# Eight tiles in place of five with a seven-product second matmul, and the scores before them moved up

## The chip, the cores and the metric

The kernel runs on one core of a Trainium2 chip. The metric is the device time of one execution in microseconds (us). Before the change three runs gave 2065.69, 2065.81 and 2067.15 us, with a median of 2065.81.

## What is computed

Four batches of channel attention feed a two-layer network. With `B, N, C = 4, 6080, 256` and `DFF = 2048`, the reference is, cut to what matters:

```python
qn = q / (norm(q, axis=1) + 1e-6)           # per batch and channel
kn = k / (norm(k, axis=1) + 1e-6)
s = kn.transpose(0, 2, 1) @ qn / tau        # C x C scores, a sum over all N rows
a = softmax(s)
x = v @ a                                   # N x C per batch
h = x @ w_in
out = maximum(0.01 * h, h) @ w_out
```

## The kernel before

**Tiles.** The rows of a batch are cut into six tiles of two halves, 512 columns a half in the first four and 496 in the last two. Tiles are numbered 0 to 23 over the batches, so batch 3 is tiles 18 to 23. Each tile runs over eight pairs of 128-wide blocks of `DFF` (`NPAIR`), numbered 0 to 7.

**First product.** `v @ (a @ w_in)` is taken in one: the 256x256 softmax is first multiplied into `w_in` (`w_pair`, then `w_parts`), and the result, split in a high and a low half, goes to DRAM (`w_dram`) and comes back pair by pair (`w_load`). Products with it are made in seven block products in place of eight (`block_product`, L1069), each in three passes of halves: 21 matmuls a pair. From tile 6 on all halves are 2-byte floats. On the way ScalarE copies a block from PSUM (`taken`, L1112) and VectorE adds a second one to it (`add`, L1106); that sum must be read out of bank `ps_z` before the next product adds to `ps_z`.

**Second product.** In plain tiles `ffn_out` (L1386) multiplies the four activated blocks of a pair by `w_out` in eight block products, 24 matmuls a pair. In the tiles of `FAST`, 18 to 22, `fast_slot` writes out a pair by hand: there the second product too is made in seven block products (`fast_out`, L1206), 21 matmuls a pair. Its operands are sums of activated blocks, which GpSimd's accumulating DMAs make (`sums_start`), and sums of blocks of `w_out`, made once into the tile `spare` (`wo_sums`). VectorE makes the low halves (`low`, L1167; in plain tiles `leaky`, L1099). A step that belongs to the next tile lies in pair 1 of such a tile: `v_scale` gathers the largest value of the next `v` (L163 to L177) and turns it into scales (`find` and `v_found`, L191 to L973).

**Scores.** Each batch's scores are summed over 48 chunks of rows while earlier tiles run. Batch 3's chunks are already scaled by the norms: `unit` on VectorE (L297), a cast to the high half on ScalarE (L302), the low half on VectorE (L306), then four matmuls (`product`, L336), two of 512 columns and two of 256, into the banks `ps_s` and `ps_y`. The norms themselves come from squares summed ahead, which fill `spare` until then. Batch 2's norms need a reciprocal of 258 columns (`wide_inverse`, L444).

**Order.** The program is one stream; each engine's own order is as recorded. Work that isn't a tile's own stands in lists per engine (`put`), and `slot(queue, room)` at fixed places of a pair records from a list what fits into `room`, an assumed length in us. Chunks, norms and sums enter the lists at pairs numbered from the start (`at`). Batch 2's scores begin at pair 48 over 28 pairs, batch 3's at pair 100 over 25 pairs; each batch's products with `w_in` follow them.

## Time and profile before

| | us |
|---|---|
| median of three runs | 2065.81 |
| profiled execution | 2066.83 |
| span of its trace | 2064.86 |
| TensorE busy | 2048.8 (99%) |
| VectorE busy | 1691.7 (82%) |
| ScalarE busy | 1496.6 (72%) |
| GpSimd busy | 256.2 (12%) |

The end of a matmul in the trace is modelled, and back-to-back matmuls overlap in it, so TensorE's busy share says only that it seldom stands. What a matmul takes is read as the distance of two starts, and what a tile loses is its length less its matmuls at these distances. A tile's length here is from the first matmul of its first pair to that of the next tile.

### The profile page before, as it was taken

What the parts mean: (1) busy time and instruction counts of PE and PEld (TensorE: products, weight loads), DVE (VectorE), ACT (ScalarE), POOL (GpSimd) and SP (SyncE); (2) the same over time, 40 slices, a digit from 0 to 9 for tenths busy, and PEclk for the clock granted to TensorE, in tenths of its full rate; (3) what the DMA queues carried; (4) which work ended last, traced back from release to release, by engine and by line L of the source; (5) the groups of instructions that cost most, each with busy time, mean ns of one, the idle gap of its engine ahead of it and who ended that gap; (6) DMA issues with size and microseconds to landing.
All of it is one profiled execution on the core that took longest, in us unless ns stands there. A gap on an engine that the chain in (4) does not pass through costs nothing.

```text
span 2064.9 us, 27776 instructions
## 1 busy us (share of the span) xinstructions
PE 2048.8 (99%) x9516; PEld 1182.9 (57%) x9516; DVE 1691.7 (82%) x3112; ACT 1496.6 (72%) x2715; POOL 256.2 (12%) x331
## 2 busy tenths in 40 slices
PE   9999999999999999999999999999999999999998
PEld 8888888888874554544444444444444444444444
DVE  8988888878788787878888878877787888988973
ACT  6577777766668888877666666666666788898874
POOL 0000000000011332220001000000010343343310
PEclk9999999999999999999999999999999999999999
DMA  9945575655575998752334323232342677677630
GB/s 371 392 169 204 199 249 204 177 177 177 205 205 165 251 254 214 208 141 92 128 129 129 113 99 127 97 115 75 103 136 98 150 144 150 136 143 147 133 66 25
DMA packets 145438, 335.37 MB, mean 162 GB/s; under 512 B 18480, under 2 KB 38832, under 8 KB 145296
## 3 DMA queue, kind: packets, MB, share of 16 engines
q1 hardware_dynamic: 105776, 251.72, 36.2%
q0 software_dynamic: 39152, 81.55, 19.2%
q8 instruction: 75, 1.23, 0.3%
q14 instruction: 67, 0.55, 0.1%
q10 hardware_dynamic: 368, 0.32, 0.0%
HBM read 221.97 MB, written 57.42 MB: 135 GB/s over the span
## 4 chain that ended last, share of the span: by engine, by line
PE 93%; DVE 4%; ACT 2%; issue 1%; DMA 0%; DVEq 0%; ACTq 0%
PE ps_o L1386 37%; PE ps_x L1069 22%; PE ps_z L1069 17%; PE ps_o L1206 5%; PE ps_s L336 4%; PE ps_o L336 2%; PE ps_y L336 2%; PE ps_s L1673 1%; PE ps_y L1206 1%; PE ps_s L1206 1%; DVE h L1106 1%; DVE g_pair L1167 1%; ACT g L1089 0%; DVE g_split L1099 0%; PE ps_y L740 0%
## 5 line engine op out<-in xcount | busy, mean ns | idle before, releaser
L1386 PE MATMUL ps_o<-g_split,w_out_split 128*128 128x512 f16 (+3 forms) x3456 | 846.5, 381 | 0.0
L1069 PE MATMUL ps_x<-v_split,w_split 128*128 128x512 f16 (+3 forms) x2280 | 619.8, 380 | 2.4 <-ACT h L1112 1.6
L1106 DVE TENSOR_TENSOR h<-ps_z,h 128x512 f32<-128x512 f32 (+1 forms) x529 | 360.6, 682 | 175.0 <-ACT h L1112 157.0
L1069 PEld LDWEIGHTS <-w_split 128*128 128x128 f16 x3024 | 292.9, 98 | 352.5 <-issue 18.1
L1099 DVE TENSOR_TENSOR g_split<-g,g_split 128x512 f16<-128x512 f32 (+3 forms) x576 | 393.6, 683 | 113.2 <-ACT g_split L1089 106.2
L1112 ACT COPY h<-ps_x 128x512 f32<-128x512 f32 (+1 forms) x537 | 308.8, 575 | 226.0 <-PE ps_x L1069 222.4
L1069 PE MATMUL ps_z<-v_split,w_split 128*128 128x512 f16 (+3 forms) x1704 | 461.5, 379 | 5.9 <-DVE h L1106 5.6
L1089 ACT ACTIVATE g<-h 128x512 f32<-128x512 f32 (+1 forms) x456 | 284.5, 624 | 202.9 <-DVE h L1106 200.4
L1386 PEld LDWEIGHTS <-w_out_split 128*128 128x128 f16 x2496 | 244.2, 98 | 288.1
L1089 ACT ACTIVATE g_split<-h 128x512 f16<-128x512 f32 (+3 forms) x432 | 263.7, 610 | 0.0
L1386 PEld LDWEIGHTS ps_o<-g_split,w_out_split 128*128 128x128 f32 x1152 | 216.3, 188 | 43.6
L1069 PEld LDWEIGHTS ps_x<-v_split,w_split 128*128 128x128 f32 x576 | 107.8, 188 | 22.4 <-ACT g L1089 0.4
L1206 PE MATMUL ps_o<-g_pair,w_out_split 128*128 128x512 f16 (+1 forms) x360 | 99.1, 378 | 0.5 <-ACT g_pair L1162 0.3
L1167 DVE TENSOR_TENSOR g_pair<-g_b,g_pair 128x512 f16<-128x512 f32 (+1 forms) x120 | 78.5, 681 | 25.5 <-ACT g_pair L1162 25.5
L1015 DVE SCALAR_TENSOR_TENSOR v_split<-v_raw,v_scale,v_split 128x512 f16<-128x512 f32 (+1 forms) x125 | 93.1, 745 | 4.1
L1089 ACT ACTIVATE g<-ps_x 128x512 f32<-128x512 f32 (+1 forms) x152 | 89.4, 588 | 7.5 <-PE ps_x L1069 5.2
L1095 ACT CAST g_split<-g 128x512 f16<-128x512 f32 (+3 forms) x144 | 88.6, 615 | 4.5
L1069 PEld LDWEIGHTS ps_z<-v_split,w_split 128*128 128x128 f32 x408 | 76.2, 188 | 16.6 <-DVE h L1106 1.4
L1206 PEld LDWEIGHTS <-spare 128*128 128x128 f16 x480 | 47.0, 98 | 56.3 <-issue 0.5
L234 POOL MEMSET qk_raw<- 64x512 f32 x5 | 2.6, 521 | 586.2 <-ACT sq L260 267.6
L270 POOL DMA_DIRECT2D spare<-sq x48 | 43.6, 908 | 221.5 <-ACT sq L269 221.3
L1162 ACT CAST g_pair<-g_b 128x512 f16<-128x512 f32 (+1 forms) x120 | 69.7, 614 | 0.0
(263 smaller groups left out, 2351.0 us busy)
## 6 DMA issues: line engine op xcount, KB each, us to landing
w_split<-w_dram SPq DMA_DIRECT2D x104, 448.0 KB, 3.9
w_split<-w_dram SPq DMA_DIRECT2D x40, 896.0 KB, 4.9
qk_raw<-in_q_dram SPq DMA_DIRECT2D x115, 256.0 KB, 4.9
qk_raw<-in_k_dram SPq DMA_DIRECT2D x115, 256.0 KB, 5.1
v_raw<-in_vT_dram SPq DMA_DIRECT2D x32, 512.0 KB, 5.0
out_dram<-o_sb SPq DMA_DIRECT2D x64, 256.0 KB, 3.3
spare<-sq POOLq DMA_DIRECT2D x47, 256.0 KB, 5.1
g_a<-g_a POOLq DMA_DIRECT2D x32, 256.0 KB, 3.2
```

The costliest lines, as they stand in the source:

```text
L336: mm = nc.tensor.matmul(out=out, lhsT=lhsT, rhs=rhs, start=start, stop=stop, skip_group_check=True)
L1015: return nc.vector.scalar_tensor_tensor(out=sp[:, 1, 0:w], in0=src, scalar=up, in1=sp[:, 0, 0:w], op0=ALU.mult, op1=ALU.subtract)
L1069: mm = nc.tensor.matmul(out=ps[:, 0:n], lhsT=w[:, x, a, :], rhs=sp[:, y, 0:n], start=first and k == 0, stop=k == 2, skip_group_check=True,)
L1089: return nc.scalar.activation(out=to, in_=h[:, 0:n], func=AF.Prelu, alpha=0.01, scale=G_SCALE if i >= T16 else 1.0)
L1095: issued["act"] = nc.scalar.copy(out=sp[:, 0, 0:n], in_=out[:, 0:n])
L1099: issued["dve"] = nc.vector.tensor_tensor(out=sp[:, 1, 0:n], in0=out[:, 0:n], in1=f32(sp[:, 0, 0:n]), op=ALU.subtract)
L1106: issued["dve"] = nc.vector.tensor_tensor(out=h[:, 0:n], in0=ps[:, 0:n], in1=h[:, 0:n], op=ALU.add)
L1112: issued["act"] = nc.scalar.copy(out=h[:, 0:n], in_=ps[:, 0:n])
L1162: return nc.scalar.copy(out=sp[:, 0, 0:n], in_=g32[i, p, HELD.get(name, name)][:, 0:n])
L1167: return nc.vector.tensor_tensor(out=sp[:, 1, 0:n], in0=g32[i, p, HELD.get(name, name)][:, 0:n], in1=sp[:, 0, 0:n], op=ALU.subtract)
L1206: issued["pe"] = nc.tensor.matmul(out=ps[:, 0:n], lhsT=fast_lhsT(i, p, prod, x), rhs=sp[:, y, 0:n], start=p == 0 and k == 0, stop=p == NPA ...
L1386: issued["pe"] = nc.tensor.matmul(out=o_ps[i][j][h][:, 0:n], lhsT=wo_lhsT(i, x, f, h), rhs=sp[:, y, 0:n], start=p == 0 and early and k == ...
```

## The change

`FAST` becomes 15 to 22: tiles 15, 16 and 17, of batch 2, now take the second product in seven block products too. In these tiles there is no slot for TensorE, so everything of batch 3 up to its products with `w_in` must stand in tiles before 15:

- batch 2's scores keep their start and are spread over 22 pairs; batch 3's have no pair of their own any more: they begin when batch 2's products with `w_in` are done and the norms are there (`start`), up to five chunks under way in place of three, and each group's load is issued when a buffer came free (`load_next`);
- batch 3's scores use one bank, so a chunk is six matmuls of 256 columns in place of two of 512 and two of 256; the same columns;
- the high halves of the products with `w_in` of batches 2 and 3 move from VectorE to ScalarE (`high`, 64 instructions), two of them share a buffer (`Splits`), and `w_pair` starts its second half before the first is split;
- `slot` carries up to 0.6 us of room to the next slot in plain tiles and looks through several lists;
- the sums of `w_out` come earlier, the last of them behind batch 3's last chunk;
- in all tiles of `FAST` the scales of the next `v` (`v_found`) are recorded at the end of pair 1, not early in it, and for tile 16 the maxima of `v` one pair sooner than they stood for tile 19.

Counted over the whole order, there are 120 matmuls of 512 columns fewer, 48 of 496 fewer and 192 of 256 more; in columns 36,096 fewer.

```diff
-SUMS_AT = (82, 84, 86, 130)
+SUMS_AT = (79, 83, 85)
+UNITS = 5
+SCORES_AT = {1: (8, 20), 2: (48, 22), 3: (0, 0)}
+NORMS_AT = 80
+EARLY = 3
...
-    FAST = range(NTILES - NT, NTILES - 1)
+    FAST = range(NTILES - NT - EARLY, NTILES - 1)
...
-            sp = work.tile([P, 2, 2, C], F16, name="qk_split", tag="qk_split", bufs=3)
+            self.at[j], sp = splits.take("qk_split")
+            sp = sp.rearrange("p (x y c) -> p x y c", x=2, y=2)
...
+                    elif len(self.s) == 1:
+                        s = self.s[0][:, h * C:(h + 1) * C]
+                        if n == 0:
+                            products += [
+                                (s, sp[:, 1, 0, hs], sp[:, 0, x, :], first and h == x == 0, False) for x in range(2)
+                            ]
+                        else:
+                            products.append((s, sp[:, 1, 1, hs], sp[:, 0, 0, :], False, last))
...
+            at(now[0] + 2, self.start)
+        def start(self):
+
+            self.starts -= 1
+            if not self.starts:
+                for j in range(NCHUNK):
+                    unit_work(self, j)
...
-                    nc.vector.tensor_scalar(out=hi, in0=src, scalar1=up, scalar2=None, op0=ALU.mult)
+                    if b < LEAN:
+                        nc.vector.tensor_scalar(out=hi, in0=src, scalar1=up, scalar2=None, op0=ALU.mult)
...
+            if b >= LEAN:
+                def high_of(n, k=k, halves=halves):
+                    at, of = ((x0, ((a11, A11, 1), (a[1], A22, 2))), (S1, ((s12, S1, 2), (s34, S3, 2))))[n]
+                    s, to = splits.take(("w_first", "w_rest")[n])
+                    to = to.rearrange("p (x s f) -> p x s f", x=2, s=4)
+                    halves[n] = s, to
+                    return high(k, [to[:, 0]], at, *of)
+
+                def low_of(n, k=k, p=p, halves=halves):
+                    at, of = ((x0, ((a11, A11, 1), (a[1], A22, 2))), (S1, ((s12, S1, 2), (s34, S3, 2))))[n]
+                    (s, to), w = halves[n], (3, 4)[n]
+                    last = split(k, [to[:, 0], to[:, 1]], at, *of)
+                    nc.gpsimd.dma_start(
+                        out=w_dram[b, p][:, :, at * P:(at + w) * P],
+                        in_=to[:, :, 0:w].rearrange("p x s f -> p x (s f)"),
+                    )
+                    splits.close(s)
+                    if n:
+                        w_done[b, p] = now[0]
+                    return last
+
+                for n in range(2):
+                    yield (0.7, 0.8)[n], lambda n=n, fn=high_of: fn(n), (0.7, 0.85)[n], lambda n=n, fn=low_of: fn(n)
+                continue
...
-        if i in FAST or i - 1 in FAST:
-            if i > FAST[0]:
+        if i // NT == B - 1:
+            if i % NT:
...
-        steps = [("dve_idle", 0.7, lambda: whole(0)), ("dve_idle", 0.7, lambda: whole(1))]
-        for name in ("low", "high"):
-            steps += [("dve_idle", 0.9, lambda n=name: sums(n)), ("act", 0.65, lambda n=name: high(n)),
-                      ("dve_idle", 0.7, lambda n=name: rest(n))]
-        return steps
+        return [("dve_idle", 0.7, lambda: whole(0)), ("dve_idle", 0.7, lambda: whole(1)), ("dve_idle", 0.9, lambda: sums("low")),
+                ("dve_idle", 0.9, lambda: sums("high")), ("act", 0.65, lambda: high("low")), ("dve_idle", 0.7, lambda: rest("low")),
+                ("act", 0.65, lambda: high("high")), ("dve_idle", 0.7, lambda: rest("high"))]
...
-        slot("dve", (3.0, 2.4, 2.3, 1.5, 1.5, 1.3, 1.3, 1.3)[p])
+        slot("dve", (3.0, 1.3, 2.3, 1.5, 1.5, 1.3, 1.3, 1.3)[p])
...
+        if i == FAST[0]:
+            slot("act", 1.4)
...
-        if wide:
-            slot("dve", 3.2 if p == 4 else 1.9)
+        if wide or p == 1:
+            slot("dve", 3.2 if p == 4 else 1.9 if wide else 1.3)
+        if i == FAST[0]:
+            slot("dve_idle", 1.4)
+            slot("act", 1.4)
...
+    carried = {"act": 0.0, "dve": 0.0, "most": 0.6}
+
     def slot(queue, room):
         engine = queue.split("_")[0]
-        while todo[queue] and todo[queue][0][0] <= room and todo[queue][0][1].ready():
-            length, fn = todo[queue].popleft()
+        lists = (queue,)
+        if queue == "act":
+            lists = ("act_first", "act")
+        if queue == "dve":
+            lists = ("dve", "dve_first", "dve_idle") if now[0] % NPAIR > 4 else ("dve_first", "dve", "dve_idle")
+        if queue in carried:
+            room += carried[queue]
...
+                    break
+            else:
+                if queue in carried and now[0] // NPAIR not in FAST:
+                    carried[queue] = min(room, carried["most"])
+                return
+            length, fn = todo[of].popleft()
...
+    def load_next(sc):
+        if sc.loaded < len(sc.groups):
+            sc.load(sc.loaded, qk_raw())
+            sc.loaded += 1
...
-        while unit_waits and len(unit_ahead) < 3:
+        while unit_waits and len(unit_ahead) < UNITS and len(unit_temps) < 3:
...
             t.append(temp(name="unit").rearrange("p (x c) -> p x c", x=2))
-            return sc.unit(j, t[0])
+            ins = sc.unit(j, t[0])
+            if j % G == G - 1:
+                load_next(sc)
+            return ins
 
         def product():
             unit_ahead.pop(0)
             unit_go(sc)
-            return sc.product(j)
-
-        put("dve", 0.7, unit, [("act", 0.6, lambda: sc.unit_high(j, t[0]), [
-            ("dve", 0.7, lambda: sc.unit_low(j, t[0]), [("pe_next", 1, product)])
-        ])])
+            splits.close(sc.at[j])
+            if j == 0:
+                sc.begin(None, bank("s"))
+            mm = sc.product(j)
+            if j == NCHUNK - 1:
+                norm_work(sc)
+                put_steps(wo_sums(NPAIR // 2 - 1), False, True)
+            return mm
+
+        def low():
+            unit_temps.remove(j)
+            unit_go(sc)
+            return sc.unit_low(j, t[0])
+
+        def high():
+            put("act", 0.6, lambda: sc.unit_high(j, t[0]), [
+                ("dve", 0.7, low, [("call", lambda: put(
+                    "pe_next", 1, product, ready=lambda: (sc.b - 1, "products") in w_done
+                ))])
+            ], ready=splits.free)
+
+        put("dve", 0.7, unit, [("call", high)])
...
-            norms = [cross[0], ("dve", 1.0, sc.unit_added), ("dve", 0.7, sc.maxima)]
+            norms = [("dve", 0.7, sc.unit_scaled), ("dve", 0.7, sc.maxima)]
...
+            if b >= LEAN:
+
+                def to(*step):
+                    put("dve_first", *step)
+
+                def halves(y):
+                    then = [("call", half_done)] if x == 0 and y is parts[-1] else []
+                    put("act", y[0], y[1], [("call", to, *y[2:], then)], ready=splits.free)
+
+                to(*parts[0])
+                to(*parts[1], [("call", lambda: [halves(y) for y in parts[2:]])])
+                return
...
+        def products_done():
+            w_done[b, "products"] = now[0]
+            if b + 1 < B:
+                for _ in range(RBUFS - 1):
+                    load_next(scores[b + 1])
+                scores[b + 1].start()
+
         def step(n):
             after = [("call", step, n + 1)] if n < 6 else [("call", half_done)]
+            if n == 6 and b >= LEAN:
+                after.append(("call", w_pair, b, q + 1) if q + 1 < NWC // 2 else ("call", products_done))
+            if n == 5 and q + 1 == NWC // 2 and b + 1 >= UNIT and b + 1 < B:
+                after.append(("call", load_next, scores[b + 1]))
...
-                ("act" if n in copies else "dve", 0.65, lambda: taken(n), after, True)
+                ("act_first" if n in copies else "dve", 0.65, lambda: taken(n), after, True)
...
-            at(w - (i in FAST) if i else 3, v_load, i + 1)
+            at(w - (i + 1 >= FAST[0]) if i else 3, v_load, i + 1)
...
+                w -= i + 1 in FAST
                 at(w + 1, v_scale_work, i + 1)
-                at(w + 3, v_go, i + 1, 3)
-                at(w + 4, v_go, i + 1, 3)
-                at(w + 5, v_go, i + 1, 3)
-                at(w + 6, v_go, i + 1, 3)
+                for n in range(3, 7):
+                    at(w + n, v_go, i + 1, 3)
+                w = i * NPAIR
...
-        begin_at, span = (NPAIR, 20) if b == 1 else (0, 28) if b < UNIT else (4, 25)
-        when = {j: w0 + begin_at + j * span // NCHUNK for j in range(NCHUNK)}
+        begin, span = SCORES_AT[b]
+        when = {j: begin + j * span // NCHUNK for j in range(NCHUNK)}
...
-        for j in range(NCHUNK):
-            at(when[j], square_work if b == 1 else chunk_work if b < UNIT else unit_work, sc, j)
-        e = w0 + begin_at + span + (1 if b < UNIT else 0)
-        at(e, norm_work, sc)
+            at(NORMS_AT, unit_norms, sc)
...
-    for m in range(NPAIR // 2):
-        at(SUMS_AT[m], lambda m=m: put_steps(wo_sums(m), False, False))
+    for m in range(NPAIR // 2 - 1):
+        at(SUMS_AT[m], lambda m=m: put_steps(wo_sums(m), False, True))
...
-            if not todo["dve"]:
-                slot("dve_idle", 0.9)
...
-            slot("pe", 0 if i or p else 2)
+            slot("act_first", 0.65)
+            slot("pe", (1 if i >= T16 else 0) if i or p else 2)
```

Two places show how the order moves. The first is VectorE in tile 20, pair 1, from the last copies of `gather` on; `h` is the block that `add` completes, `g_pair` and `g_t` are halves for the second product. Before:

```order
L177 COPY zeros<-zeros 32x1 x3
L191 TENSOR_REDUCE v_scale<-zeros 32x1
L193 COPY v_scale<-v_scale 32x1 x3
L196 TENSOR_SCALAR v_scale<-v_scale 128x1
L197 TENSOR_SCALAR v_scale<-v_scale 128x1
L200 TENSOR_SCALAR v_scale<-v_scale 128x1
L204 TENSOR_SCALAR v_scale<-v_scale 128x1
L973 TENSOR_SCALAR v_scale<-v_scale,rest_down 128x1 x2
L1167 TENSOR_TENSOR g_pair<-g_b,g_pair 128x512 x2
L1106 TENSOR_TENSOR h<-ps_z,h 128x512
```

After (line numbers are the changed kernel's: `add` is L1200, `low` L1261):

```order
L181 COPY zeros<-zeros 32x1 x3
L1261 TENSOR_TENSOR g_pair<-g_b,g_pair 128x512 x2
L1200 TENSOR_TENSOR h<-ps_z,h 128x512
L1261 TENSOR_TENSOR g_pair<-g_a,g_pair 128x512
L1261 TENSOR_TENSOR g_t<-g_a,g_t 128x512
L1200 TENSOR_TENSOR h<-ps_z,h 128x512
L1261 TENSOR_TENSOR g_t<-g_b,g_t 128x512
L1261 TENSOR_TENSOR g_pair<-g_b,g_pair 128x512
L1261 TENSOR_TENSOR g_pair<-g_a,g_pair 128x512
L195 TENSOR_REDUCE v_scale<-zeros 32x1
L197 COPY v_scale<-v_scale 32x1 x3
```

The scales (from L191 before, L195 after) stood ahead of the pair's two additions and now stand behind both.

The second place is VectorE in tile 9, pair 6, up to the second addition; `ny<-nt` is the reciprocal of batch 2's norms, `v_split` a half of the next `v`. Before:

```order
L1099 TENSOR_TENSOR g_split<-g,g_split 128x512 x2
L1106 TENSOR_TENSOR h<-ps_z,h 128x512
L1012 TENSOR_SCALAR v_split<-v_raw,v_scale 128x496
L1015 SCALAR_TENSOR_TENSOR v_split<-v_raw,v_scale,v_split 128x496
L1099 TENSOR_TENSOR g_split<-g,g_split 128x512
L1012 TENSOR_SCALAR v_split<-v_raw,v_scale 128x496
L1015 SCALAR_TENSOR_TENSOR v_split<-v_raw,v_scale,v_split 128x496
L1012 TENSOR_SCALAR v_split<-v_raw,v_scale 128x496
L1015 SCALAR_TENSOR_TENSOR v_split<-v_raw,v_scale,v_split 128x496
```

After:

```order
L1193 TENSOR_TENSOR g_split<-g,g_split 128x512
L491 RECIPROCAL ny<-nt 128x258
L494 TENSOR_SCALAR rk<-ny,rtau 128x2
L1193 TENSOR_TENSOR g_split<-g,g_split 128x512
L1200 TENSOR_TENSOR h<-ps_z,h 128x512
L1106 TENSOR_SCALAR v_split<-v_raw,v_scale 128x496
L1109 SCALAR_TENSOR_TENSOR v_split<-v_raw,v_scale,v_split 128x496
L1193 TENSOR_TENSOR g_split<-g,g_split 128x512
L1106 TENSOR_SCALAR v_split<-v_raw,v_scale 128x496
L1109 SCALAR_TENSOR_TENSOR v_split<-v_raw,v_scale,v_split 128x496
L1106 TENSOR_SCALAR v_split<-v_raw,v_scale 128x496
L1109 SCALAR_TENSOR_TENSOR v_split<-v_raw,v_scale,v_split 128x496
```

The reciprocal, which stood in tile 10, now stands in this pair beside the same splits of `v`.

## Rows read from the trace of the kernel before

**Rows 1.** The page of the profiled execution: engines, and the chain that ended last.

```profile
PE 2048.8 (99%) x9516; PEld 1182.9 (57%) x9516; DVE 1691.7 (82%) x3112; ACT 1496.6 (72%) x2715; POOL 256.2 (12%) x331
...
PE 93%; DVE 4%; ACT 2%; issue 1%; DMA 0%; DVEq 0%; ACTq 0%
```

**Rows 2.** Windows from tile start to tile start: tiles 10 to 13, 16 to 19.

```profile
core 0: us, PE busy (x) PEld busy (x) DVE busy (x) ACT busy (x) POOL busy (x), PEclk, DMA share, GB/s
...
941.58:1022.53 80.95, 80.59 (x387) 37.73 (x385) 67.29 (x131) 54.77 (x105) 1.44 (x2) 1.00 0.30 98
1022.53:1103.00 80.47, 80.47 (x385) 37.58 (x384) 68.63 (x150) 51.89 (x97) 6.91 (x10) 1.00 0.40 138
1103.00:1185.67 82.67, 81.46 (x381) 37.12 (x380) 72.88 (x144) 55.88 (x102) 4.01 (x6) 1.00 0.38 114
1185.67:1273.12 87.45, 87.45 (x421) 41.12 (x420) 70.42 (x119) 58.73 (x107) 0.00 (x0) 1.00 0.32 109
...
1447.16:1527.57 80.41, 80.23 (x382) 37.24 (x381) 62.83 (x126) 52.53 (x99) 3.37 (x5) 1.00 0.35 109
1527.57:1607.56 79.99, 79.99 (x382) 37.27 (x381) 64.98 (x136) 51.65 (x96) 5.39 (x8) 1.00 0.37 123
1607.56:1675.76 68.20, 66.11 (x299) 28.97 (x298) 56.71 (x113) 55.83 (x102) 22.86 (x28) 1.00 0.68 148
1675.76:1749.28 73.52, 72.68 (x337) 32.83 (x336) 65.36 (x120) 62.49 (x115) 28.80 (x33) 1.00 0.72 144
```

**Rows 3.** Timeline of TensorE: products of 512, 256 and 496 columns, starts first.

```profile
1275.93 0.27 PE L336 MATMUL ps_s<-qk_split 128*128 128x256 f16 x1
1276.04 0.27 PE L336 MATMUL ps_y<-qk_split 128*128 128x256 f16 x1
1276.14 0.38 PE L336 MATMUL ps_s<-qk_split 128*128 128x512 f16 x1
...
1280.47 1.89 PE L1386 MATMUL ps_o<-g_split,w_out_split 128*128 128x512 f16 x8
1282.19 0.81 PE L1069 MATMUL ps_x<-v_split,w_split 128*128 128x512 f16 x3
...
1544.96 1.84 PE L1386 MATMUL ps_o<-g_split,w_out_split 128*128 128x496 f16 x8
1546.63 0.79 PE L1069 MATMUL ps_x<-v_split,w_split 128*128 128x496 f16 x3
```

**Rows 4.** Timeline of tile 19, pairs 1 and 2: VectorE and TensorE, idle in brackets.

```profile
1689.03 0.14 DVE L191 TENSOR_REDUCE v_scale<-zeros 32x1 f32<-32x4 f32 x1
...
1690.33 0.34 DVE L973 TENSOR_SCALAR v_scale<-v_scale,rest_down 128x1 f32<-128x1 f32 x2
...
1691.78 0.68 DVE L1106 TENSOR_TENSOR h<-ps_z,h 128x512 f32<-128x512 f32 x1
...
1692.52 0.81 PE L1069 MATMUL ps_z<-v_split,w_split 128*128 128x512 f16 x3 [0.84 <-DVE h L1106]
...
1699.81 0.69 DVE L1106 TENSOR_TENSOR h<-ps_z,h 128x512 f32<-128x512 f32 x1 [0.28 <-ACT h L1112]
...
1700.93 0.81 PE L1069 MATMUL ps_z<-v_split,w_split 128*128 128x512 f16 x3
```

**Rows 5.** Timeline of tile 12, pair 4: VectorE, ScalarE and TensorE.

```profile
1148.07 0.68 DVE L297 TENSOR_TENSOR unit<-qk_raw,spare 128x512 f32<-128x512 f32 x1
1148.79 0.62 ACT L302 CAST qk_split<-unit 128x512 f16<-128x512 f32 x1 [2.21 <-DVE unit L297]
1149.32 0.58 ACT L1112 COPY h<-ps_x 128x512 f32<-128x512 f32 x1
...
1149.94 0.81 PE L1069 MATMUL ps_x<-v_split,w_split 128*128 128x512 f16 x3 [0.71 <-ACT h L1112]
```

**Rows 6.** Groups by line of VectorE, 941 to 1010 us: tile 10's reciprocal.

```profile
L444 DVE RECIPROCAL ny<-nt 128x258 f32<-128x258 f32 x1 | 1.8, 1756 | 0.0
```

**Rows 7.** Timeline of VectorE, tile 18, pair 1: the next tile's maxima.

```profile
1618.15 2.46 DVE L158 TENSOR_REDUCE v_scale<-v_raw 128x1 f32<-128x512 f32 x4
```

More of the change, by code (lines that the diff above doesn't have):

```diff
@@ L206, in find, with __init__, free, take @@
             )
+    class Splits:
+        def __init__(self):
+            self.open, self.half = [], None
+        def free(self, whole=False):
+            return self.half is not None and not whole or sum(1 for n in self.open[-3:] if n) < 3 and not (
+                len(self.open) >= 3 and self.open[-3]
+            )
+        def take(self, name):
+            assert self.free()
+            if self.half is None:
+                self.open.append(2)
+                self.half = work.tile([P, 2, 4 * P * 2], F16, name=name, tag="qk_split", bufs=3)
+                return len(self.open) - 1, self.half[:, 0]
+            to, self.half = self.half, None
+            return len(self.open) - 1, to[:, 1]
+        def whole(self, shape, name):
+            if self.half is not None:
+                self.half = None
+                self.open[-1] -= 1
+            assert self.free(True)
+            self.open.append(1)
+            return len(self.open) - 1, work.tile(shape, F32R, name=name, tag="qk_split", bufs=3)
+        def close(self, n):
+            self.open[n] -= 1
+    splits = Splits()
     def m_tile():
@@ L775, in w_parts, with high @@
         two = "p (s f) -> p s f"
+        def high(k, to, at, *blocks):
+            for src, x0, n in blocks:
+                src = src[:, k * P:(k + 1) * P] if n == 1 else src.rearrange(two, s=2)[:, :, k * P:(k + 1) * P]
+                hi = to[0][:, x0 - at, :] if n == 1 else to[0][:, x0 - at:x0 - at + n, :]
+                last = nc.scalar.activation(out=hi, in_=src, func=AF.Copy, scale=2.0**-TOP)
+            return last
         def split(k, to, at, *blocks):
@@ L1684, in taken @@
             if n == 0:
-                for name in ("c11", "c21", "c12", "c22"):
-                    c[name] = w_tmp("w_a")
+                for x, name in enumerate(("c11", "c21", "c12", "c22")):
+                    if not chained:
+                        c[name] = w_tmp("w_a")
+                    elif x % 2 == 0:
+                        c["two"] = work.tile([P, 2, TW], F32, name="w_c", tag="v_split", bufs=VBUFS)
+                    if chained:
+                        c[name] = c["two"][:, x % 2, :]
             if n in copies:
```

114 lines of the change are left out of this document (73 added, 41 removed).

## The prediction

> **What bounds the kernel now.** The page comes first: TensorE is busy 99% of the span, and 93% of the chain that ended last is its own work [rows 1]. But those bars overlap, so the windows by tile come next, against what the matmuls of a tile need. A 512-column product starts 0.215 us after the one before it (eight in 1.72 us), a 496-column one 0.209 us (eight in 1.67 us), a 256-column one 0.11 us [rows 3]. Tile 13 has 360 products of 512 columns and 15 chunks of scores: 360 x 0.216 + 30 x 0.216 + 30 x 0.109 = 87.5 us, and it is 87.45 us long [rows 2]. So TensorE runs at its distance there, and nothing else costs anything, although VectorE is busy 70.42 us. I take 0.216, which that tile confirms. The same sum for other tiles gives what each loses: tile 10 0.6 us, tile 11 0.2, tile 12 1.8, tile 16 0.5, tile 17 0.2, tile 18 4.2 (273 x 0.216 + 24 x 0.209 = 64.0 against 68.20), tile 19 0.9 (336 x 0.216 = 72.6 against 73.52) [rows 2]; tiles 20 to 22 are like 19, tiles 13 to 15 lose nothing. The clock stands at 1.00 in all of these rows, its level of 2.4 GHz. So the time changes in two ways: by products that go away, and by what the tiles lose when VectorE or ScalarE come late.
>
> **The products.** A tile that joins `FAST` has 168 in place of 192 matmuls in its second product. Tile 15 is 512 wide, 16 and 17 are 496 wide: 24 x 0.216 + 48 x 0.209 = 15.2 us less, all on TensorE's own chain, with no cover to lose. A check: tile 13 without its scores is 77.7 us and tile 19 without its loss 72.6, so a seven-product tile is worth 5.1 us, 24 x 0.213. The chunks of batch 3 have 96 fewer of 512 columns and 192 more of 256: two of 0.109 for one of 0.216, +0.2 us over all. Each 256-column product now has another behind it with weights of its own; two stand so in each chunk already, 0.11 us apart [rows 3], so the loads stay hidden. Products: **-15.0 us**.
>
> The Trainium skill (TensorE: Matmul & The Clock Gate, Back-to-back issue gap) gives 215.7 ns for a product of 512 columns by itself and about 131 ns in a stream with weight loads; by the second figure 72 products would be an estimated 9.4 us, and the time 2056 us. The trace has streams with loads at 0.215 us, so the measurement decides.
>
> **Tiles 9 to 14, where the moved work goes.** What twelve tiles (6 to 17) carried beside their own work stands in nine. I summed VectorE's instructions of each tile of the new order at the mean duration of their kind in the trace, and took 0.91 of the sum, since they overlap by that much in tiles 10 to 12 (67.29, 68.63 and 72.88 us busy [rows 2] against sums of 73.1, 76.3 and 79.9). Against TensorE's need in that tile this gives busy shares of 84% in tile 9, 87%, 90%, 84%, 85% and 83% in tile 14. Before, tiles at 83% and 85% (10, 11) lost 0.6 and 0.2 us, the one at 88% (12) lost 1.8 [rows 2]. So I take 0.4 us for tiles 12, 13 and 14, 1.0 for tile 10, 1.8 for tile 11. Tile 9 gets 1.5: the reciprocal of 1.76 us [rows 6] comes into a pair with three split steps, and pairs 5 and 6 there hold some 1.9 us more of VectorE than of TensorE. Sum 5.5 us against 2.6 before: **+2.9 us**. Ends: no loss at all, -2.6; every tile like tile 12, 6 x 1.8 - 2.6 = +8.2. ScalarE gets the 64 high halves, but has 25 us free in tiles 10 to 12 [rows 2]; nothing for it.
>
> **Tiles 15 to 22.** The first tile of `FAST` lost 4.2 us as tile 18. TensorE's pairs 1 to 3 are short there, since the second product lags, and VectorE had to take the next tile's maxima, 2.46 us [rows 7], and its scales in the same pairs. For tile 16 the maxima stand sooner: by the same sums VectorE's work in pairs 1 and 2 falls from 15.3 us in tile 18 to 11.8 us in tile 15, against 13.0 us of TensorE. So the part that came from VectorE's load goes, some 2 us, and the waits on ScalarE stay: 2.2 us, between 1.0 (an inner tile) and 4.2. Tile 18 becomes an inner tile of `FAST`. These lose 0.9 us at one point: in pair 1, VectorE does gather and scales back to back, its addition comes at 1691.78, and TensorE's `ps_z` stands 0.84 us for it [rows 4]. Scales moved behind the additions free 1.6 us (1689.03 to 1690.6), so this wait goes. But they then stand ahead of pair 2's first addition. That one had 0.28 us of idle time before it and ended 0.37 us before TensorE needed it (1700.93 less 1700.50, less 0.06 of handing over) [rows 4]; with TensorE 0.9 to 1.0 us ahead, about 0.35 us of the wait comes back one pair later, and 0.1 more because VectorE now idles for ScalarE in pair 1. I take 0.45 us a tile, between 0 and 0.95. So: tiles 15 to 17 from 0.7 (tiles 16 and 17) to 2.2 + 2 x 0.45 = 3.1, **+2.4**; tile 18 from 4.2 to 0.6, **-3.6** (it starts wider than tile 17 and needs one addition more); tiles 19 to 22 4 x (0.45 - 0.95), **-2.0**. The 96 more accumulating DMAs stand on GpSimd's queue, which is busy 28.8 of 73.5 us in such a tile [rows 2], with the stores of `w_dram` gone from it by then; nothing. Tile 23 isn't touched.
>
> **The sum.** -15.0 + 2.9 + 2.4 - 3.6 - 2.0 = -15.3 us. The profiled execution took 2066.83 us, which becomes 2051.5; the median of the runs is 1.0 below it, so 2050.5 us. With all ends taken low: -15.0 - 2.6 + 0.3 - 4.2 - 3.8 = -25.3, so 2040.5; all high: -15.0 + 8.2 + 5.4 - 3.3 = -4.7, so 2061.1.
>
> **Rivals.** A measurement of this kernel can tell about 0.2%, 4.1 us, from no change.
>
> *The waits go too.* Carried room and two lists by rank let VectorE keep up; tiles 9 to 14 lose nothing, and the scales moved behind pair 1 cost nothing. For it: tiles 13 to 15 lose nothing at 80%. Against it: pairs 5 and 6 of tile 9. Time: -15.0 - 2.6 + 1.0 - 3.6 - 3.8, some -24, to -20 if half of it holds: 2042 to 2046.
>
> *The waits come back.* Tiles 9 to 14 each like tile 12, tile 15 like tile 18, and 0.95 us in each later tile: 2058 to 2061, still faster by more than 0.2%, or just at it.
>
> *In-order hand-offs cost more than the products saved.* In tile 12 ScalarE stands 2.21 us in front of a cast whose `unit` VectorE hadn't done yet; behind the cast waits the copy of a block, and TensorE stands 0.71 us for that copy [rows 5]. The new order has more such triples (VectorE, ScalarE, VectorE) in each of tiles 9 to 14, chunks and high halves alike. The Trainium skill (the same page, the section on the 16 sub-arrays) has ScalarE's and VectorE's queues as strictly first in, first out, TensorE's alone able to pull weight loads ahead; rows 5 agree. The gain without these tiles is 15.0 + 3.6 + 2.0 us; over nine tiles, 9 to 17, with 3.3 us lost in them before, this is used up at 2.7 us a tile. With tile 18's 4.2 us in each it is 9 x 4.2 - 3.3 - 20.6 = +14, 2080 us. Against it: no plain tile lost over 1.8 us.
>
> That the products don't go away is no rival, since the order shows them gone.
>
> **How the numbers follow.** Forecast, 2046 to 2056: 0.63. Waits go too: 0.14. Waits come back: 0.17, a third of it beyond 2061.7 and so within 0.2%. Slower: 0.04, and 0.02 for something between it and no change. Faster by over 0.2%: 0.63 + 0.14 + 0.12 = 0.89; within 0.2%: 0.07; slower: 0.04. The range leaves out half of the low rival and the end of the high one: 2043 to 2059.
>
> **What would show it.** Right: tiles 15 to 17 of 73 to 70 us (15 shorter, as part of its products runs later), tiles 19 to 22 near 73.0, plain tiles 10 to 14 at TensorE's need and 0.4 to 1.8 us; pair 1 of a `FAST` tile without its 0.84 us, pair 2 with some 0.3 us of it. Wrong: a tile from 9 to 14 that loses over 3 us, TensorE idle behind `unit`, `high` or a load of `qk_raw`, or chunks of six products longer than 0.66 us.

## The result, and the profile after

The forecast was wrong in sign. The changed kernel takes 2091.4 us (median of four runs, 2087.6 to 2094.3) against 2066.0 for the kernel before: a ratio of 1.012, 95% interval 1.0107 to 1.0132, some 25 us slower where 15 us faster was forecast. The profiled execution took 2090.67 us, its span is 2088.9 us, 24.0 longer than before.

The page of the changed kernel, engines and the chain of waits, answers to [rows 1]:

```profile
PE 2046.9 (98%) x9540; PEld 1184.8 (57%) x9540; DVE 1720.7 (82%) x3143; ACT 1548.8 (74%) x2849; POOL 339.1 (16%) x427
...
PE 81%; DVE 9%; ACT 5%; DMA 3%; issue 2%; POOL 0%; SPq 0%; DVEq 0%; ACTq 0%; POOLq 0%
```

The busy bars hardly moved. The chain did: 93% of it was TensorE's own work, now 81%, and VectorE, ScalarE and DMA hold 17% in place of 6%. So TensorE stands more, and the windows by tile (columns as in [rows 2]; tiles 7, 10 to 14, 16 to 19 of the changed kernel) say where:

```profile
690.54:784.46 93.92, 90.17 (x421) 45.32 (x420) 73.20 (x123) 75.43 (x140) 27.95 (x39) 0.98 0.88 223
...
960.47:1050.85 90.38, 85.75 (x405) 39.52 (x404) 73.81 (x151) 61.19 (x123) 6.23 (x9) 1.00 0.54 144
1050.85:1143.64 92.79, 86.50 (x439) 43.38 (x438) 74.91 (x139) 60.54 (x120) 6.10 (x9) 0.96 0.39 131
1143.64:1235.26 91.62, 91.03 (x482) 46.97 (x481) 77.01 (x130) 60.97 (x111) 0.00 (x0) 1.00 0.37 122
1235.26:1328.42 93.16, 90.58 (x464) 45.34 (x463) 78.91 (x144) 62.33 (x117) 0.52 (x1) 1.00 0.27 87
1328.42:1418.55 90.13, 86.99 (x394) 38.83 (x393) 70.27 (x141) 62.87 (x131) 10.20 (x15) 0.98 0.38 119
...
1486.11:1557.50 71.39, 70.92 (x338) 32.87 (x336) 64.09 (x120) 61.09 (x115) 27.91 (x32) 1.00 0.92 197
1557.50:1628.81 71.31, 70.64 (x338) 32.87 (x337) 64.20 (x120) 60.68 (x115) 27.63 (x32) 1.00 0.94 212
1628.81:1703.48 74.67, 72.93 (x337) 32.78 (x337) 65.43 (x121) 62.21 (x115) 28.27 (x33) 1.00 0.76 156
1703.48:1776.62 73.14, 72.69 (x338) 32.83 (x337) 65.43 (x120) 62.45 (x115) 28.35 (x33) 1.00 0.72 145
```

Lengths can't be compared row by row, since scores moved between tiles. What each tile loses can: every start of a matmul less the start before it, less the distances of [rows 3] (and those of the 4-byte matmuls of tiles 0 to 5, read in the same way: 0.227 us for 512 columns, 0.222 for 496, 0.216 between two of 256), summed where more than 0.06 us is left. What is lost just before a tile's first matmul counts to the tile before it:

| tiles, us lost | before | after |
|---|---|---|
| 0 / 1 to 5 | 1.6 / 1.0 | 6.0 / 4.1 |
| 6 / 7 / 8 | 1.9 / 1.5 / 1.6 | 2.1 / 7.1 / 1.8 |
| 9 / 10 / 11 | 1.2 / 0.5 / 0.4 | 5.7 / 5.4 / 8.9 |
| 12 / 13 / 14 | 1.8 / 0.0 / 0.0 | 1.0 / 3.2 / 5.3 |
| 15 / 16 / 17 / 18 | 0.0 / 0.4 / 0.2 / 4.3 | 3.5 / 0.7 / 1.0 / 2.6 |
| 19 to 22, each | 1.0 | 0.6 |
| 0 to 23 | 22.5 | 62.9 |

40 us more are lost; less the 15 us of products that is the 25 us of the result. (The two spans are only 24.0 us apart, since the last store landed in 2.1 us, in 4.0 before.) What TensorE waited for is a view of its own (line, releaser: us in total, times, longest). Before:

```profile
PE ps_z L1069 <- DVE h L1106: 5.6, 9, 0.8
PE ps_x L1069 <- ACT h L1112: 1.6, 4, 0.7
```

After (L1838 and L329 are products with `w_in` and the norms' sum, which wait for the sum L1860 that empties a bank; L624 turns the softmax):

```profile
PE ps_z L1163 <- DVE h L1200: 14.6, 16, 6.2
PE ps_x L1163 <- ACT h L1206: 8.2, 8, 3.7
PE ps_s L1838 <- DVE w_a L1860: 4.5, 4, 2.0
PE ps_y L329 <- DVE w_a L1860: 2.3, 1, 2.3
PE ps_s L624 <- DVE s_sb L615: 1.9, 1, 1.9
PE ps_s L624 <- DVE s_cross L615: 1.4, 1, 1.4
...
PE ps_s L1838 <- DVE w_c L1860: 1.0, 2, 0.7
```

Additions and copies came late for 15.6 us more, and TensorE stood 11.1 us in front of moved steps of its own, in front of which it had not stood before. Four places show the kinds.

**Tile 11: a round trip that lost its slack.** The maxima of the next `v` go to DRAM and back to reach all partitions. Timelines of SP's queue, the store and the load behind it, before and then after:

```profile
1037.94 0.33 SPq L166 DMA_DIRECT2D v_scale_line<-v_scale  x1
1045.42 0.33 SPq L186 DMA_DIRECT2D zeros<-v_scale_line  x1
```

```profile
1077.46 0.33 SPq L170 DMA_DIRECT2D v_scale_line<-v_scale  x1
1086.99 0.32 SPq L190 DMA_DIRECT2D zeros<-v_scale_line  x1
```

The store left 15.4 us after the tile's start before, and 26.6 after: the maxima stood in a list behind split steps that are looked at first. The scales kept their place in pair 3. VectorE got to them at 1084.3, before the load was even issued. Timelines of VectorE and TensorE:

```profile
1092.53 0.29 DVE L199 TENSOR_REDUCE v_scale<-zeros 128x1 f32<-128x128 f32 x1 [8.22 <-DMA zeros<-v_scale_line]
...
1097.28 1.40 PE L1163 MATMUL ps_z<-v_split,w_split 128*128 128x496 f16 x3 [6.24 <-DVE h L1200]
```

And windows of 1 us there (columns as in [rows 2], the granted clock third from the end):

```profile
1094.00:1095.00 1.00, 0.00 (x0) 0.00 (x0) 0.96 (x3) 0.00 (x0) 0.00 (x0) 1.00 0.00 0
1095.00:1096.00 1.00, 0.00 (x0) 0.00 (x0) 0.96 (x3) 0.00 (x0) 0.00 (x0) 0.52 0.00 0
...
1100.00:1101.00 1.00, 1.00 (x4) 0.34 (x3) 1.00 (x3) 1.00 (x4) 0.00 (x0) 0.50 0.54 111
...
1102.00:1103.00 1.00, 1.00 (x6) 0.49 (x5) 0.33 (x2) 0.57 (x1) 0.00 (x0) 1.00 0.58 233
```

An addition that stands behind the scales on VectorE holds TensorE 6.24 us. Then its granted clock is 0.50 until 1101.9, its level of 1.2 GHz, which costs the tile about 2 us more.

**Tile 10: a product close behind its sum.** Timelines of VectorE and TensorE:

```profile
1009.11 0.68 DVE L1193 TENSOR_TENSOR g_split<-g,g_split 128x496 f16<-128x496 f32 x1
1009.70 1.38 DVE L1130 TENSOR_TENSOR v_raw<-v_raw 128x496 f32<-128x496 f32 x2
1011.00 0.68 DVE L1860 TENSOR_TENSOR w_a<-w_a,ps_s 128x512 f32<-128x512 f32 x1
...
1011.73 0.81 PE L1838 MATMUL ps_s<-win,aT 128*128 128x512 f16 x3 [1.72 <-DVE w_a L1860]
```

VectorE doesn't idle in these lines. It does two sums for the next `v`, which could have waited, and then the one that TensorE stands for; with that sum in front (e4) this wait is gone.

**Tile 7: a buffer that a store still holds.** ScalarE's copy needs a buffer from which a result is being stored (timelines of ScalarE and TensorE):

```profile
722.24 0.59 ACT L1206 COPY h<-ps_x 128x512 f32<-128x512 f32 x1 [4.25 <-DMA out_dram<-o_sb]
...
722.88 1.36 PE L1163 MATMUL ps_x<-v_split,w_split 128*128 128x512 f16 x3 [3.75 <-ACT h L1206]
```

The four stores were issued from 702.8 to 707.7, 14 us and more before. The DMA view of that tile (KB each, median us to landing) shows how slow a transfer is there, before and then after:

```profile
v_scale_line<-v_scale SPq DMA_DIRECT2D x1, 0.5 KB, 9.4
```

```profile
v_scale_line<-v_scale SPq DMA_DIRECT2D x1, 0.5 KB, 12.4
```

**Tile 0: room that was carried.** A conversion of weights, filled into carried room, waits for VectorE and holds ScalarE's copy:

```profile
100.23 0.72 ACT L707 ACTIVATE f_scale<-f_scale,exp_bias 128x512 int32<-128x512 int32 x1 [2.69 <-DVE f_scale L701]
...
102.51 0.97 PE L1163 MATMUL ps_x<-v_split,w_split 128*128 128x512 f32 x3 [1.82 <-ACT h L1206]
```

### The profile page after: what moved, and what is told of

Same layout as the page of the kernel before. It is cut to its first block, busy times and chain, and to the rows that moved or that the text cites. A ratio compares the mean times of both kernels' runs of the same rounds, so it can differ in the third digit from the quotient of the medians.

```text
span 2088.9 us, 28180 instructions
## 1 busy us (share of the span) xinstructions
PE 2046.9 (98%) x9540; PEld 1184.8 (57%) x9540; DVE 1720.7 (82%) x3143; ACT 1548.8 (74%) x2849; POOL 339.1 (16%) x427
## 4 chain that ended last, share of the span: by engine, by line
PE 81%; DVE 9%; ACT 5%; DMA 3%; issue 2%; POOL 0%; SPq 0%; DVEq 0%; ACTq 0%; POOLq 0%
PE ps_o L1485 26%; PE ps_x L1163 20%; PE ps_z L1163 15%; PE ps_o L1300 8%; PE ps_s L385 4%; DVE h L1200 2%; PE ps_o L385 2%; PE ps_y L1300 2%; PE ps_s L1300 2%; ACT g L1183 1%; DVE g_split L1193 1%; PE ps_s L1838 1%; ACT g_split L1183 1%; DVE g_pair L1261 1%; DMA out_dram<-o_sb 1%
## 5 line engine op out<-in xcount | busy, mean ns | idle before, releaser
L1485 PE MATMUL ps_o<-g_split,w_out_split 128*128 128x512 f16 (+3 forms) x2880 | 713.0, 383 | 0.2 <-ACT o_sb L1504 0.2
L1200 DVE TENSOR_TENSOR h<-ps_z,h 128x512 f32<-128x512 f32 (+1 forms) x505 | 344.6, 682 | 183.7 <-ACT h L1206 152.2
L1193 DVE TENSOR_TENSOR g_split<-g,g_split 128x512 f16<-128x512 f32 (+3 forms) x480 | 328.8, 685 | 75.4 <-ACT g_split L1183 71.0
L1183 ACT ACTIVATE g<-h 128x512 f32<-128x512 f32 (+1 forms) x384 | 239.9, 625 | 177.5 <-DVE h L1200 174.8
L1183 ACT ACTIVATE g_split<-h 128x512 f16<-128x512 f32 (+3 forms) x360 | 220.1, 611 | 0.0
L1261 DVE TENSOR_TENSOR g_pair<-g_b,g_pair 128x512 f16<-128x512 f32 (+1 forms) x192 | 125.3, 680 | 41.5 <-ACT g_pair L1256 41.3
L1300 PE MATMUL ps_o<-g_pair,w_out_split 128*128 128x512 f16 (+1 forms) x576 | 157.9, 376 | 0.4 <-ACT g_pair L1256 0.3
L1300 PEld LDWEIGHTS <-spare 128*128 128x128 f16 x768 | 75.1, 98 | 88.9 <-issue 0.4
L1256 ACT CAST g_pair<-g_b 128x512 f16<-128x512 f32 (+1 forms) x192 | 111.0, 611 | 0.0
L1261 DVE TENSOR_TENSOR g_pair<-g_a,g_pair 128x512 f16<-128x512 f32 (+1 forms) x128 | 86.7, 677 | 1.4 <-ACT g_pair L1256 1.0
```

The source lines that it names most:

```text
L1183: return nc.scalar.activation(out=to, in_=h[:, 0:n], func=AF.Prelu, alpha=0.01, scale=G_SCALE if i >= T16 else 1.0)
L1193: issued["dve"] = nc.vector.tensor_tensor(out=sp[:, 1, 0:n], in0=out[:, 0:n], in1=f32(sp[:, 0, 0:n]), op=ALU.subtract)
L1200: issued["dve"] = nc.vector.tensor_tensor(out=h[:, 0:n], in0=ps[:, 0:n], in1=h[:, 0:n], op=ALU.add)
L1256: return nc.scalar.copy(out=sp[:, 0, 0:n], in_=g32[i, p, HELD.get(name, name)][:, 0:n])
L1261: return nc.vector.tensor_tensor(out=sp[:, 1, 0:n], in0=g32[i, p, HELD.get(name, name)][:, 0:n], in1=sp[:, 0, 0:n], op=ALU.subtract)
L1300: issued["pe"] = nc.tensor.matmul(out=ps[:, 0:n], lhsT=fast_lhsT(i, p, prod, x), rhs=sp[:, y, 0:n], start=p == 0 and k == 0, stop=p == NPA ...
```

## The experiments

Each is an edit of the changed kernel. Ratios are to the kernel before on the same chip; 0.1% is 2.1 us.

**The moved work alone** (e1).

```
-EARLY = 3
+EARLY = 0
```

> The changed kernel with its whole moved order, but with FAST at 18 to 22 as before: the moved work alone, without its gain. Theory (the 72 products fewer are worth their 15.0 us, and the moved work costs some 40 us in waits of TensorE in tiles 0 to 15): tile 15 to 17 are plain again and lose nothing, so 15.0 us more than the changed kernel's 2091.4, less the 3.5 us that tile 15 lost as the first of FAST, plus 1.4 for tile 18 as the first again: 2104 us (2100 to 2109). Rival (the seven-product tiles 15 to 17 are no faster than plain ones, since the accumulating DMAs collide with other transfers there): no more than 2093 us.

2095.1 us, ratio 1.0152 (1.0137 to 1.0167). The moved work without its gain costs 31 us, some 7 us more than with it by the ratios: above the rival, but below the theory's range too, whose 2104 was too high. Tiles 15 to 18 of its trace take 77.70 + 75.46 + 75.30 + 68.52 = 297.0 us and lose 4.6; in a second profile of the changed kernel (e5) they take 67.55 + 71.39 + 71.59 + 74.68 = 285.2 and lose 8.1. So the products give 11.8 + 3.4 = 15.2 us, as forecast. The rest of the miss is elsewhere: tile 14 is 3.2 us shorter without `FAST` behind it, and tiles that have the same order differ by up to 1.7 us between two executions (next run).

**The changed kernel again** (e5), unaltered.

> The changed kernel once more, unaltered, to tell what its waits do from execution to execution, beside its variants. Theory (the waits for transfers differ from execution to execution, those for sums and for the softmax don't): 2087 to 2094 us, tile 7 anywhere from 88 to 95 us (93.9, 94.5, 90.7 and 89.0 us in four profiles with the same order up to there), tile 10 within 0.5 us of 90.4, tile 14 of 88.4 to 90.1. Rival (all of it is set by the order): every tile within 0.5 us of the changed kernel's first profile.

2090.7 us (2085.8 to 2091.3), ratio 1.0115 (1.0100 to 1.0130). Tile 10 took 90.41 and tile 14 90.13 us, as in the first profile (90.38, 90.13), so the waits for sums and softmax belong to the order. Neither expectation holds in full. Tile 7 took 93.69 us (93.92 in the first), but tile 0 took 99.06 (97.50) and tile 9 85.72 (87.41), and these two don't differ by a transfer. TensorE stands 1.87 us for the softmax in tile 9 in both traces, and only in the first does the granted clock fall behind it. Timeline of TensorE and a window of 2 us, first profile and then e5:

```profile
950.89 0.72 PE L624 MATMUL ps_s<-ident,s_sb 128*128 128x128 f32 x4 [1.87 <-DVE s_sb L615]
953.00:955.00 2.00, 2.00 (x6) 0.66 (x5) 1.04 (x3) 1.41 (x4) 0.00 (x0) 0.50 0.00 0
```

```profile
952.01 0.72 PE L624 MATMUL ps_s<-ident,s_sb 128*128 128x128 f32 x4 [1.87 <-DVE s_sb L615]
954.00:956.00 2.00, 2.00 (x11) 0.88 (x9) 1.16 (x3) 1.31 (x4) 0.00 (x0) 1.00 0.00 0
```

In tile 0 it is the other way round: TensorE stands 1.82 us in both, and the clock falls to 0.50 for 3.4 us in e5 only. So a comparison of single tiles over two traces can be off by 1.7 us through the clock alone.

**No carried room before tile 6** (e2).

```
-                    carried[queue] = min(room, carried["most"])
+                    carried[queue] = min(room, carried["most"] if now[0] >= T16 * NPAIR else 0.0)
```

> The changed kernel, but room is carried from slot to slot only from tile 6 on, so tiles 0 to 5 fill their slots by the room alone. Theory (carried room puts work of VectorE ahead of an addition or a copy, and tiles 0, 3, 4 and 5 lose 14.1 us over the distance of their matmuls in place of 6.2 before): these four tiles fall back to some 6 to 7 us, 2084 us (2082 to 2087). Rival (they lose it by the other edits there, the lists by rank and the slots taken out, or by the order further back): tiles 0 to 5 keep their lengths within 1 us, 2090 to 2092.

2079.2 us, ratio 1.0073 (1.0058 to 1.0088). Tiles 0 to 5 take 510.7 us, as before the change (510.7; 518.5 with it). The theory holds for these tiles: carried room alone cost them 7.8 us, and the other edits there nothing. The whole fell below its range (2082 to 2087): in this trace tile 7, behind them, is 3.5 us shorter too, while tile 10 is 3.9 longer.

**The maxima of `v` in front** (e3).

```
-        put("dve", 0.2, lambda: v_scale[i].gather(), (), True)
+        put("dve_first", 0.2, lambda: v_scale[i].gather(), (), True)
```

(and the four maxima likewise)

> The changed kernel, but the four maxima of the next v and their gathering go to the front of the list that is looked through first. Theory (in tile 11 the gathering slid from pair 1 to pair 2, 26.5 us into the tile, was 15.4 before, while the scales kept their place in pair 3, so the way through DRAM of 9.1 and 5.5 us is waited for, TensorE stands 6.4 us and then runs at half its clock for some 5 us): the wait goes, tile 11 falls by 7 to 9 us, 2083 us (2081 to 2086). Rival (the way through DRAM is slow there because of other transfers, whenever it begins; or the maxima in front hold up the additions just as long): the wait stays at 3 us or more or comes up in another tile, 2088 to 2092.

2084.6 us, ratio 1.0100 (1.0083 to 1.0117). Half each. The wait is gone, and tile 11 falls by 7.7 us, as the theory has it. But the tiles beside it grow, as in the rival's last words (its windows of tiles 10 to 12):

```profile
956.13:1049.57 93.44, 87.45 (x406) 39.96 (x405) 73.80 (x151) 61.21 (x123) 6.20 (x9) 0.98 0.50 139
1049.57:1134.69 85.12, 83.76 (x434) 42.23 (x432) 74.58 (x139) 59.86 (x119) 6.10 (x9) 1.00 0.40 137
1134.69:1230.50 95.81, 93.38 (x487) 47.94 (x486) 78.41 (x134) 62.83 (x114) 0.00 (x0) 0.98 0.35 116
```

In tile 12 ScalarE now waits 3.56 us for a result's store, as in tile 7.

**The sums of the products in front** (e4).

```
-                ("act_first" if n in copies else "dve", 0.65, lambda: taken(n), after, True)
+                ("act_first" if n in copies else "dve_first", 0.65, lambda: taken(n), after, True)
```

> The changed kernel, but the sums that take the products with w_in out of PSUM on VectorE go to the front of the list that is looked through first. Theory (TensorE waits 7.8 us in seven places for such a sum, 2.0 us at the longest, and pays about as much again at half its clock behind the waits of 2 us; the sum stands behind work that can wait): these waits fall to under 3 us, and tiles 10 and 14 by 3 us each, 2085 us (2082 to 2088). Rival (the products are put into TensorE's order too close behind their sums, at a third place in a pair, so that no order on VectorE brings the sum in time): the waits stay at 6 to 9 us, 2089 to 2093.

2082.6 us, ratio 1.0094 (1.0074 to 1.0115). Products no longer show among the long waits, the norms' sum keeps its 2.3 us. The theory's size is right, its tiles are not: tile 11 fell by 9.7 us, because the maxima came earlier in this order too (their store leaves 17.9 us after the tile's start, not 26.6, and the scales stand for no transfer), while tile 13 grew by 3.8. So this run doesn't price the sums alone.

**The loads of batch 3's scores on GpSimd's queue** (e6).

```
-            sc.load(sc.loaded, qk_raw())
+            sc.load(sc.loaded, qk_raw(), (nc.gpsimd, nc.gpsimd), False)
```

(cut; `load` takes the new argument)

> The changed kernel, but the loads of batch 3's scores are issued on GpSimd's queue in place of SP's. Theory (on SP's queue such a load waits for the scaling that frees its buffer, up to 10.0 us, and holds up what stands behind it: the stores of results, whose buffers ScalarE's copies need, and the gathering of the scales; TensorE stands for that in tile 13, pair 1, 1.1 us, and in tile 11): tiles 11 and 13 fall by 2 to 9 us together, 2086 us (2081 to 2090). Rival (the loads don't hold up anything that is needed, the transfers themselves are slow): tiles 11 to 13 keep their lengths within 1 us in sum, 2089 to 2093.

2090.3 us, ratio 1.0119 (1.0104 to 1.0134); tiles 11 and 13 kept 92.67 and 93.31 us. The rival's range: in the changed kernel such a load waits up to 10.9 us at the head of SP's queue, but what stands behind it isn't what TensorE lacks.

**The third place for products later** (e7): its `slot` moved behind the last two block products of a pair.

> The changed kernel, but the third place in a pair at which a product with w_in may enter TensorE's order, new with the change, comes two block products later (six matmuls, 1.3 us). Theory (at the place where it is, a product stands right behind the sum that frees its bank, and TensorE waits for VectorE or ScalarE): part of the 7.8 us of waits for such sums goes, 2087 us (2083 to 2090). Rival (the waits belong to the two older places as well; at the second one TensorE stood 1.9 us in tile 10): no more than 1 us less in tiles 9 to 14, 2089 to 2093.

2082.2 us, ratio 1.0068 (1.0051 to 1.0086). More than expected: waits for the sums at L1838 fall from 5.5 to 2.4 us, tiles 10, 13 and 14 by 1.3, 1.8 and 4.2 us against e5. The profiled execution (2086.0 us) was the slowest of its four, so the trace shows less than the median gained. In it a wait that was small before has grown at the end of tile 17, where ScalarE stands for an accumulating DMA of a `FAST` tile, and TensorE for ScalarE:

```profile
1622.32 0.60 ACT L1256 CAST g_t<-g_a 128x496 f16<-128x496 f32 x1 [3.02 <-DMA g_a<-g_b]
...
1623.96 0.81 PE L1163 MATMUL ps_x<-v_split,w_split 128*128 128x512 f16 x3 [2.34 <-ACT g_a L1244]
```

At this place TensorE lost 0.3 us in the first profile of the changed kernel and up to 2.5 in those of its variants. DMA is busiest there (0.94 in the row of tile 17 above).

**Five edits at once** (e8): e2, e3, e4, e6, e7.

> The changed kernel with five of these edits at once: no carried room before tile 6, maxima of v in front, sums of the products in front, loads of batch 3 on GpSimd's queue, the third place two block products later. Theory (the waits are separate and each edit takes away its own): 12 us by the carried room, 7 by the maxima, 9 by the sums (2091.4 less what each gave alone), and 2 to 5 by the other two, so 2056 to 2062 us, below the kernel before. Rival (VectorE and ScalarE are too full in tiles 9 to 14, and a wait that is taken away in one place comes up in another, as tile 10 or 12 grew when tile 11 fell): 2068 us or more.

2071.9 us (2068.7 to 2074.6), ratio 1.0027 (1.0017 to 1.0036): in the rival's range, 10 us above the theory's. The waits are separate in part only: by their ratios, less than e5's 1.0115, the five gave 4 + 2 + 2 + 0 + 5 tenths of a per cent one by one, against some 0.9% together. That VectorE and ScalarE are too full, the rival's reason, isn't shown by it. What is left has a cause of the order as well, which e4's trace shows too:

```profile
1118.51 0.62 ACT L343 CAST qk_split<-unit 128x512 f16<-128x512 f32 x1 [3.65 <-DMA w_dram<-w_rest]
```

The order counted a buffer of two high halves as free once its store was issued, and ScalarE stands until the store has landed.

**Three edits more** (e9): that buffer counts as free four block products later, batch 3's norms come four pairs sooner, and room is carried from tile 9 on only.

```
-NORMS_AT = 80
+NORMS_AT = 76
...
-                    splits.close(s)
+                    closing.append((beats[0] + 4, s))
```

> The version with five edits, and three more for the waits that its trace still shows: batch 3's norms four pairs sooner, so that their matmul doesn't stand among the products with w_in (2.6 us in tile 10); a buffer of two high halves counts as free four block products after its last store was issued, not at once (ScalarE waited 3.1 us for such a store in the kernel with the sums in front, and TensorE 2.6 us in tile 11 and 2.4 in tile 14 in the version with five); room is carried from tile 9 on only. Theory (these waits are separate too, and each of 2 us costs about as much again at half the clock): tiles 10, 11 and 14 fall by 3 to 4 us each, tiles 7 and 8 by up to 3, from 2071.9 to 2058 us (2055 to 2063), below the kernel before. Rival (VectorE and ScalarE have no room left there, and what is taken away comes up elsewhere): 2067 us or more.

2061.6 us (2057.7 to 2064.9) against 2065.2, ratio 0.9979 (0.9970 to 0.9987): 0.2% faster than the kernel before. The result lies in the theory's range, 3.6 us above its 2058, and speaks against the rival of this run and the last. Its waits of TensorE:

```profile
PE ps_z L1166 <- DVE h L1203: 7.1, 14, 1.0
PE ps_x L1166 <- ACT h L1209: 6.4, 8, 2.8
PE ps_x L1166 <- ACT g_a L1247: 1.7, 1, 1.7
...
PE ps_s L624 <- DVE s_sb L615: 0.5, 1, 0.5
```

Tile 11 now loses nothing, tile 10 3.8 us and tile 14 2.0; the 2.8 us is tile 7's, which didn't fall (92.8 us, 91.2 in e8). In all tiles e9 loses 35.0 us, 12.5 more than the kernel before, so most of the 15 us of products is still spent.

**Two tiles in place of three** (e10): e9 with `EARLY = 2`.

> The same version with FAST at 16 to 22, so that tile 15 is plain and two tiles join in place of three. Theory (a tile that joins gives 5.1 us by its 24 products, whoever is first in FAST pays 3.5 us): 5.1 us above the version with three, within 1 us. Rival (the third tile presses the next v and the moved work of tile 14 together and gives less than it takes): level with the version with three, or below it.

2066.1 us (2063.8 to 2073.2), ratio 1.0009 (1.0000 to 1.0018): 4.5 us above e9. The theory: a tile that joins is worth its products. By the traces tiles 14 to 17 together are 5.3 us longer than in e9.

**Batch 2's scores over 24 and 26 pairs** (e11, e12): e9 with `2: (48, 24)` and `2: (48, 26)`.

> The version with eight edits, with batch 2's scores spread over 24 pairs in place of 22 (28 before the change); all that follows them keeps its place. Theory (in tile 7 a load of the scores stands among the stores of tile 6's results on SP's queue, the last store takes 14.0 us to land, 6.7 before the change, and its buffer is the one that ScalarE's copy in pair 2 needs; with fewer chunks to a pair the load comes in another place and fewer buffers are taken between): TensorE's wait of 2.9 us in tile 7, pair 2, goes, tile 7 falls from 92.8 to 88 to 89 us, 2057.5 us (2055 to 2060). Rival (GpSimd's accumulating transfers alone fill the queues there, whatever the scores load): tile 7 stays at 92 us or more, 2060 to 2063.

> The same with batch 2's scores over 26 pairs; its norms, softmax and products then come one pair later, batch 3's end stays before tile 15 by two pairs less. Theory: tile 7 as with 24 pairs or better, 88 us; tiles 13 and 14 within 1 us of the version with 22 pairs: 2057.5 us (2055 to 2060). Rival (later products with w_in press on the split of the next v in tile 14): tile 14 loses 2 us and more over its 88.2, which takes back what tile 7 gives, 2060 to 2063.

2061.2 us (ratio 0.9980, 0.9971 to 0.9989) and 2064.3 us (0.9995, 0.9986 to 1.0004). With 24 pairs the expectation failed: the load still stood among the four stores of tile 6's results on SP's queue, the copy waited 3.74 us, and tile 7 took 91.7 us. With 26 pairs the stores follow each other and land within 5.9 us (14.0 in e9), and tile 7 takes 88.1 us:

```profile
692.95 2.34 SPq L1515 DMA_DIRECT2D out_dram<-o_sb  x4
700.15 0.33 SPq L170 DMA_DIRECT2D v_scale_line<-v_scale  x1
```

So this wait goes with the load's place, as far as these two runs tell (e12 loads less in these pairs as well). But e12's trace loses most of it again elsewhere: tile 7 is 4.6 us shorter than in e9, tiles 8, 9 and 11 are 1.6, 1.2 and 2.3 us longer, and the theory had looked at 13 and 14 alone. Its median lies above both ranges. Its profiled execution (2060.8 us) was the fastest of its eleven, so the trace doesn't show where the others lose 3.5 us more, and that stays open.

## Why the prediction was wrong

- **Products, -15.0 us: right.** e1 against e5 gives 15.2, e10 against e9 4.5 us for a tile with its other losses. The Trainium skill's 131 ns (TensorE: Matmul & The Clock Gate, Back-to-back issue gap) would have given 9.4; the measurement decides.
- **Tiles 9 to 14, +2.9 us: the step that failed.** Measured is 29.5 - 3.9 = +25.6 us. (The 2.6 us that the forecast took for before left out tile 9, which lost 1.2.) I sized each tile by VectorE's busy share of the time that TensorE needs, and these shares came out as forecast: 89% in tile 11 (74.91 us of 92.79 less 8.9), 85% in tile 12 and 83% in tile 14, for 90, 84 and 83. What failed is the step from the share to the loss. Tile 14, the least full of the six, lost 5.3 us, tile 12 1.0, and tile 11 8.9 in place of 1.8. In e9 tile 11 is fuller still, VectorE 75.35 of 81.86 us or 92%, and loses nothing (its window, columns as in [rows 2]):

```profile
1035.34:1117.20 81.86, 81.86 (x421) 41.09 (x420) 75.35 (x148) 61.01 (x126) 13.73 (x22) 1.00 0.44 137
```

What counted was for whom VectorE was working when TensorE stood. I read the new order for how much it holds and not for the distance between a step and the step that needs it.
- **"ScalarE ...; nothing for it", and tiles 0 to 8 not costed: failed.** Tiles 0 to 8 lose 21.1 in place of 7.6 us; 7.8 of the difference come by carried room (e2) and 5.6 in tile 7, where a copy waits for a store. The sum had no term for these tiles. The diff of `slot` showed that every plain tile's order changes; I counted tiles with moved work only.
- **Tiles 15 to 17, +2.4; tile 18, -3.6; tiles 19 to 22, -2.0: right in kind, short in size.** Measured are +4.6, -1.7 and -1.7. Tile 15 lost 3.5 us (2.2 forecast), tile 18 2.6 (0.6 forecast), and the accumulating DMAs that I had put at nothing make a wait of up to 2.5 us at the end of tile 17 (e7). In tile 19 pair 1 lost its 0.84 us and pair 2 waits 0.45, as forecast, against [rows 4]:

```profile
1722.49 0.14 DVE L195 TENSOR_REDUCE v_scale<-zeros 32x1 f32<-32x4 f32 x1
...
1728.26 0.81 PE L1163 MATMUL ps_z<-v_split,w_split 128*128 128x512 f16 x3 [0.45 <-DVE h L1200]
```

- **The rival on the slower side was the case.** It gave 2.7 us a tile over tiles 9 to 17 as the point where the gain is used up; they lost 34.7 / 9 = 3.9. Its price, 2080 us, was still 11 short. Its chance of 0.04 rested on "no plain tile lost over 1.8 us", which is about the old order and was no evidence on a new one. Nor was its mechanism quite the one: ScalarE's waits for `unit` [rows 5] became fewer (10.9 us in tiles 6 to 14 before, 3.7 after, by its waits from 600 to 1420 us), and the losses came from a round trip, from products close behind their sums, from stores that hold buffers, from carried room, and from the half clock behind some of these stands.
